# C v of a Nystrom attention in 64x32 tiles, each head by itself, in two parts a batch, under a newly planned order

## The chip, the cores and the metric

One core of a Trainium2 chip. The time is that of the core in device microseconds (us), from three runs, of which the median is given. One execution more was taken by the hardware profiler; its span runs from the first to the last instruction of the program. The engines are PE (TensorE, with PEld for its weight loads), DVE (VectorE), ACT (ScalarE), POOL (GpSimd) and SP (SyncE, which here only issues DMAs). Each takes its instructions in program order from a queue of its own.

## The reference

Batch 8, 8 heads, 576 positions of 64. Landmarks are means over 18 neighbouring positions, 32 per head. A = softmax(q k_lm'), B = softmax(q_lm k_lm'), C = softmax(q_lm k'), each over its last axis.

```python
Z = Bm.transpose(0, 1, 3, 2) / (norm1(Bm) * norminf(Bm) + 1e-06)   # over the last two axes
for _ in range(6):
    Z = 2 * Z - Z @ Bm @ Z
attn = A @ Z @ C @ v                       # 8 x 8 x 576 x 64
x = attn.transpose(0, 2, 1, 3).reshape(4608, 512)
out = ((x @ w1) * (x @ w2) @ w3) @ w_out   # 4608 x 512, float32
```

## The kernel before, in words

**Stages.** Heads are taken four at a time ("quads", two a batch, 16 in all). For a quad, POOL loads k and q as float16 (`lq`), DVE transposes them (`T`), the means go to `mk` and `lt` (PE for the first two quads, POOL for the rest: `ma`, `mb`). `S` is the product of q_lm and k with its softmax in `sm`, `sw`, `sb`, `se`; `ct` transposes its exponentials into `ecT`. `A` is the product of q and k_lm, with its softmax in `ar`, `am`, `as`, `ae`, `au`, `an`; `aT` is its transpose. Per group of one or two batches `N`, `x`, `Z` do the iteration of the reference.

**C v.** Per batch, `C` (`cv_mm`, L647) multiplies `ecT` by v (float32, loaded by SP as `lv` into `vb`). The 576 keys lie in two halves of 32 partitions a head and nine chunks; a product contracts 64 partitions. Two heads stand beside one another: the 64 columns of the weights are the 32 landmarks of two heads, and the streamed 128 columns are v of the same two heads. So of the 64x128 result only the two blocks of a head with itself are of use. Four such products, of two quads and two pairs, lie on the four 64x64 tiles of the array and in two PSUM banks. A tenth step multiplies the row sums of the exponentials by `unit64`, a scaled identity. `co` (`cv_out`, L665) divides by the sums and writes `cv` to SBUF. `W` (L755) multiplies `cv` by Z's block matrix; its view of `zb` takes the heads of each half in turn. `wp` and `wq` split W's result into two float16 parts and `U` multiplies it by w1 and w2, so that the two products with x become products `d` of aT with `u`.

**The dense part.** w3 and w_out are multiplied beforehand into `w34` (`mm`, 64 tasks of three products, after loads `w3n`, `wf` and splits `wh`, `wl`, `woh`, `wol`). `d` (16 matmul and weight-load instructions) gives both factors, `e` on ACT copies one, `f` on DVE multiplies. `g` (two halves of 8 instructions a tile of output) multiplies by w34, `h` on ACT copies, `st` on SP stores. `wu0` to `wu3` are six products each without use, at the start.

**The order.** The text `ORDER` (L39) names every task once, in the order in which its instructions are written to the engines' queues; behind a colon stand the buffers (PSUM banks, SBUF slots) that the task takes. It is the output of a planner that isn't in the file. What is left of it are the arguments of `add`: the planned occupation of the engine, the needs (`deps`), the buffers taken and given back (`acq`, `rel`), and `n`, the number of PE instructions. They don't change the program that is built from a given text, except through `acq`, which say which buffer a number belongs to.

A float32 product is two pairs of records in the trace (a weight load and a matmul each), a float16 product one pair.

## Time and profile before

| | |
|---|---|
| three runs | 277.85, 283.53, 285.95 us; median 283.53 |
| profiled execution | 276.25 us |
| its span | 274.5 us |
| PE busy | 93% of the span, 3948 matmul records |
| PE weight loads | 61% |
| DVE busy | 71% |
| ACT busy | 59% |
| POOL busy | 48% |
| C's products with v | 576 records, 272 ns each |

Busy shares are unions of the records of an engine. Matmuls are pipelined and lie over one another, so a record's length is longer than its share of the engine's time: what a stretch of PE's work takes is read from the start of its first record to the start of the next task's. "Issue" as the cause of an idle time means that nothing the profile shows was waited for. The granted TensorE clock was 0.995 over the span.

### The profile page before, as it was taken

The page shows a single profiled execution, that of the slowest core. Times are in us where ns is not written, and L with a number is a line of the kernel's source. Part 1 is how long each engine was busy: PE and PEld are TensorE (multiplying, and loading weights), DVE is VectorE, ACT ScalarE, POOL GpSimd, SP SyncE. Part 2 cuts the span into 40 slices and gives each one's busy share as a digit, 9 for nine tenths or more (in the row PEclk, how much of TensorE's full clock was granted, in tenths as well). Part 3 has the DMA queues.
Part 4 walks back from the last instruction along what each step waited for, and adds up shares of the span by engine and source line. Part 5 has one row for each costly group of instructions (what it writes and reads, how often), then busy time and mean ns, then how long its engine had stood idle before and what let it go on. Part 6 is the DMA issues. An engine that isn't in the chain of part 4 may idle for free.

```text
span 274.5 us, 9549 instructions
## 1 busy us (share of the span) xinstructions
PE 255.6 (93%) x3948; PEld 167.4 (61%) x3948; DVE 194.2 (71%) x470; ACT 161.3 (59%) x414; POOL 132.8 (48%) x147
## 2 busy tenths in 40 slices
PE   0958999999999899979999999999999999999993
PEld 0424444444658775568876647878866687557762
DVE  4489999999999999979999876757461255124330
ACT  0364563466477656969767799815129674485541
POOL 4006899999999889988979733000110000000000
PEclk9999999999999999999999999999999999999998
DMA  7997999999996964910476645254113210503636
GB/s 178 285 223 161 186 238 227 235 255 215 226 213 148 233 121 75 199 48 2 73 124 161 162 108 148 57 138 116 39 41 91 68 42 0 135 3 87 146 90 142
DMA packets 22668, 37.33 MB, mean 136 GB/s; under 512 B 3552, under 2 KB 7904, under 8 KB 22624
## 3 DMA queue, kind: packets, MB, share of 16 engines
q1 hardware_dynamic: 15920, 23.80, 35.2%
q0 software_dynamic: 5696, 11.54, 23.8%
q10 hardware_dynamic: 1008, 1.38, 1.7%
q8 instruction: 31, 0.51, 0.8%
q14 instruction: 13, 0.11, 0.1%
HBM read 38.80 MB, written 9.44 MB: 176 GB/s over the span
## 4 chain that ended last, share of the span: by engine, by line
PE 75%; DMA 16%; DVE 4%; issue 2%; ACT 1%; SPq 0%; DVEq 0%; ACTq 0%
PE bank L243 75%; DMA w3n<-in_moe_w_dram 13%; DMA u<-in_moe_w_out_dram 3%; DVE bank L325 1%; DVE tiny L498 1%; DVE w3t L340 1%; DVE ea L541 1%; DVE T L432 0%; ACT wo L314 0%; ACT lm L468 0%; DVE tiny L547 0%; DVE tiny L567 0%; ACT ec L517 0%; DVE T L474 0%; SPq L306 0%
## 5 line engine op out<-in xcount | busy, mean ns | idle before, releaser
L872 DVE TENSOR_TENSOR ab<-asb,bank 128x384 f16<-128x384 f16 x96 | 49.9, 544 | 38.8 <-ACT asb L866 38.3
L243 PE MATMUL bank<-aT,u 128*128 128x192 f16 x768 | 71.5, 246 | 0.0
L243 PE MATMUL bank<-w,ab 128*128 128x512 f16 (+1 forms) x296 | 69.9, 374 | 0.0
L243 PEld LDWEIGHTS <-u 128*128 128x128 f16 x768 | 63.6, 98 | 8.9 <-issue 1.3
L866 ACT CAST asb<-bank 128x384 f16<-128x384 f32 x96 | 44.1, 488 | 37.4 <-PE bank L243 29.4
L243 PE MATMUL bank<-wo,w3t 128*128 128x512 f16 x192 | 46.2, 379 | 3.7 <-ACT wo L314 2.3
L447 POOL TENSOR_TENSOR ls<-ls 128x128 f32<-128x128 f32 (+2 forms) x56 | 40.8, 729 | 4.0
L243 PEld LDWEIGHTS <-ab 128*128 128x128 f16 x296 | 27.6, 99 | 23.8 <-issue 0.7
L791 ACT CAST u<-bank 128x512 f16<-128x512 f32 x64 | 34.6, 615 | 5.7 <-PE bank L243 5.6
L581 POOL TENSOR_TENSOR ah<-ea,tiny 128x576 f16<-128x576 f32 x16 | 18.6, 1163 | 37.5 <-DVE aT L590 34.8
L440 POOL TENSOR_TENSOR ls<-nat 128x1152 f32<-128x1152 f16 x14 | 33.3, 2381 | 1.5 <-issue 1.0
L243 PEld LDWEIGHTS <-w3t 128*128 128x128 f16 x192 | 17.7, 99 | 23.8 <-issue 6.1
L886 ACT ACTIVATE osb<-bank 128x512 f32<-128x512 f32 x35 | 21.1, 607 | 16.9 <-PE bank L243 15.9
L553 POOL TENSOR_TENSOR ea<-ea,tiny 128x608 f32<-128x608 f32 x16 | 19.8, 1239 | 9.4 <-DVE tiny L547 4.8
L432 DVE STREAM_TRANSPOSE T<-nat 128x576 f32<-128x576 f32 x32 | 24.0, 751 | 0.1
L243 PE MATMUL bank<-T 32*32 32x288 f16 (+1 forms) x320 | 19.0, 291 | 0.7 <-DVE T L474 0.5
L517 ACT ACTIVATE ec<-bank,tiny 128x288 f32<-128x288 f32 x32 | 16.0, 504 | 5.2 <-DVE tiny L509 5.2
L243 PE MATMUL bank<-vb,ecT 64*64 64x128 f32 x576 | 18.3, 272 | 0.0
L243 PE MATMUL bank<-xz 32*32 32x64 f32 (+1 forms) x768 | 17.2, 214 | 1.1 <-issue 1.0
L243 PEld LDWEIGHTS bank<-vb,ecT 64*64 64x64 f32 x576 | 16.5, 133 | 1.9 <-ACT ec L517 0.9
L243 PEld LDWEIGHTS bank<-xz 32*32 32x32 f32 x768 | 12.9, 104 | 7.4 <-issue 4.2
L243 PE MATMUL bank<-w,wT 64*32 64x512 f16 x512 | 17.1, 379 | 0.0
(77 smaller groups left out, 296.0 us busy)
## 6 DMA issues: line engine op xcount, KB each, us to landing
vb<-in_v_dram SPq DMA_DIRECT2D x64, 144.0 KB, 3.9
out_dram<-osb SPq DMA_DIRECT2D x70, 128.0 KB, 2.4
nat<-in_k_dram POOLq DMA_DIRECT2D x16, 288.0 KB, 6.9
nat<-in_q_dram POOLq DMA_DIRECT2D x16, 288.0 KB, 7.5
w3n<-in_moe_w_dram SPq DMA_DIRECT2D x30, 128.0 KB, 8.0
w<-in_moe_w_dram POOLq DMA_DIRECT2D x4, 512.0 KB, 14.4
u<-in_moe_w_out_dram SPq DMA_DIRECT2D x4, 128.0 KB, 7.1
u<-in_moe_w_out_dram ACTq DMA_DIRECT2D x4, 128.0 KB, 7.2
```

What stands on the lines that cost most here:

```text
L243: nc.tensor.matmul(out_, lhsT, rhs, start=start, stop=stop, **({} if pos is None else {"tile_position": pos}))
L325: nc.vector.transpose(out=bank(at(f"w3f{j}{h}")).rearrange("p (e g i) -> p g e i", e=4, g=4), in_=w3n[at(f"w3n{j}")].rearrange("p g (e x) ...
L432: nc.vector.transpose(out=Ts[at(f"T{n}")][:, GRP * t:GRP * t + GRP] .rearrange("p r l e -> p (r l e)").bitcast(FP32), in_=nats[at(f"nat{n} ...
L440: nc.gpsimd.tensor_tensor(out=l, in0=nat[:, :, 0:9, :], in1=nat[:, :, 9:18, :], op=ALU.add)
L447: nc.gpsimd.tensor_tensor(out=l[:, :, x:x + m, :], in0=l[:, :, x:x + m, :], in1=l[:, :, y:y + m, :], op=ALU.add)
L517: nc.scalar.activation(out=ecs[at(f"ec{n}")][:, hp, :], in_=two(f"pS{n}")[hp][:, 0:288], func=AXF.Exp, scale=SCALE, bias=t[:, 2 + hp:3 + h ...
L553: nc.gpsimd.tensor_tensor(out=ea, in0=ea, in1=tinies[at(f"ta{n}")][:, 0:19].unsqueeze(2).to_broadcast([128, 19, M]), op=ALU.subtract)
L581: nc.gpsimd.tensor_tensor(out=ahs[at(f"ah{n}")].rearrange("p g m r -> p g r m"), in0=eas[at(f"ea{n}")][:, 0:GRP, :].rearrange("p (g r) m - ...
L791: nc.scalar.copy(out=uu[at(f"u{b}{qd}")][:, wi, 512 * half:512 * half + 512], in_=bank(at(f"pU{b}{wi}{half}{qd}")))
L866: nc.scalar.copy(out=asb[at(f"as{b}{j}{ch}")], in_=d1_ps(b, j, ch)[0])
L872: nc.vector.tensor_mul(abts[at(f"ab{i // 2}")][:, 2 * j:2 * j + 2, CH * (i % 2):CH * (i % 2) + CH], asb[at(f"as{b}{j}{ch}")], d1_ps(b, j, ...
L886: nc.scalar.activation(out=osb[at(f"os{i}")], in_=bank(at(f"pE{i}")), func=AXF.Copy, scale=2.0 ** -12)
```

## The change

C is computed head by head: weights of 32 columns, 64 streamed columns of v, eight products a step on the eight 64x32 tiles. The useless blocks fall away, the number of products doubles. The ten steps are written as two tasks, `Cba` (steps 0 to 4) and `Cb` (5 to 9), which the order may set apart; both use the same two banks. `cv` and `unit64` have half the width, `co` multiplies 64 columns instead of 128, and `W` is two products of 128 streamed columns instead of four of 64, without the reordering view. `ORDER` is a new text from beginning to end: 1336 words instead of 1328, with other places for the loads, the warm-up products and nearly all other tasks, and other buffers. Some of the planner's figures changed too (occupations of `wu`, `C`, `co`; DMA times of `lq` and `lw`).

```diff
-    cvs = slots(fixed, 2, [128, 2, 2, D], FP32, "cv")
+    cvs = slots(fixed, 2, [128, 2, D], FP32, "cv")
-    unit64 = fixed.tile([128, 64], FP32, name="unit64")
+    unit64 = fixed.tile([128, 32], FP32, name="unit64")
...
-    def cv_mm(b):
+    def cv_mm(b, c0, c1):
         def fn():
             ps = two(f"pC{b}")
-            for c in range(NC9 + 1):
+            for c in range(c0, c1):
                 for qd in range(2):
                     n = 2 * b + qd
                     for h2 in range(2):
-                        r, o = slice(64 * (h2 ^ qd), 64 * (h2 ^ qd) + 64), 64 * h2
-                        if c < NC9:
-                            mm(ps[qd][o:o + 64, 0:128],
-                               ecTs[at(f"ecT{n}")][r, c, :, :].rearrange("p a m -> p (a m)"),
-                               vbs[at(f"vb{n}")][r, :, c, :],
-                               start=(c == 0), stop=(c == NC9 - 1), pos=(r.start, o))
-                        else:
-                            mm(ps[qd][o:o + 64, 128:130], unit64[r, :], tinies[at(f"mx{n}")][r, 4:6],
-                               pos=(r.start, o))
+                        r = slice(64 * (h2 ^ qd), 64 * (h2 ^ qd) + 64)
+                        for a in range(2):
+                            o = 64 * h2 + 32 * a
+                            if c < NC9:
+                                mm(ps[qd][o:o + 32, 0:D], ecTs[at(f"ecT{n}")][r, c, a, :], vbs[at(f"vb{n}")][r, a, c, :],
+                                   start=(c == 0), stop=(c == NC9 - 1), pos=(r.start, o))
+                            else:
+                                mm(ps[qd][o:o + 32, D:D + 1], unit64[r, :], tinies[at(f"mx{n}")][r, 4 + a:5 + a],
+                                   pos=(r.start, o))
...
-                rc = tinies[at(f"tc{b}")][:, 2 * qd:2 * qd + 2]
-                nc.vector.reciprocal(out=rc, in_=ps[:, 128:130])
-                nc.vector.tensor_tensor(out=cvs[at(f"cv{b}")][:, qd],
-                                        in0=ps[:, 0:128].rearrange("p (a d) -> p a d", a=2),
-                                        in1=rc.unsqueeze(2).to_broadcast([128, 2, D]), op=ALU.mult)
+                nc.vector.reciprocal(out=t[:, qd:qd + 1], in_=ps[:, D:D + 1])
+                nc.vector.tensor_tensor(out=cvs[at(f"cv{b}")][:, qd], in0=ps[:, 0:D],
+                                        in1=t[:, qd:qd + 1].to_broadcast([128, D]), op=ALU.mult)
...
-            for x in range(2):
-                for s in range(2):
-                    zb = zbs[at(f"zb{i}")][:, 2 * b - 2 * GROUPS[i][0] + s, :, :]
-                    mm(ps[64 * s:64 * s + 64, 0:128].rearrange("p (e a m) -> p a e m", e=2, a=2)[:, x], cvs[at(f"cv{b}")][:, s, x, :],
-                       zb.rearrange("p (e a) m -> p a e m", a=2)[:, x], pos=(0, 64 * s))
+            for s in range(2):
+                mm(ps[64 * s:64 * s + 64, 0:128], cvs[at(f"cv{b}")][:, s, :],
+                   zbs[at(f"zb{i}")][:, 2 * b - 2 * GROUPS[i][0] + s, :, :].rearrange("p h m -> p (h m)"), pos=(0, 64 * s))
...
-        add(f"C{b}", "PE", 2.2, cv_mm(b), deps=[f"ct{n0}", f"ct{n1}", f"lv{n0}", f"lv{n1}", "cc"],
-            acq=both(f"pC{b}", 1),
+        add(f"C{b}a", "PE", 0.89, cv_mm(b, 0, 5), deps=cvd, acq=both(f"pC{b}", 1),
             rel=[f"ecT{n0}", f"ecT{n1}", f"vb{n0}", f"vb{n1}", f"mx{n0}", f"mx{n1}"],
-            at=(p, 2.0), mode="64x64", kind="C", n=160)
+            at=(p, 2.0), mode="64x32", kind="C", n=160)
+        add(f"C{b}", "PE", 0.89, cv_mm(b, 5, 10), deps=[f"C{b}a"],
+            rel=[f"ecT{n0}", f"ecT{n1}", f"vb{n0}", f"vb{n1}", f"mx{n0}", f"mx{n1}"],
+            at=(p, 2.1), mode="64x32", kind="C", n=160)
```

The new order around C1, C2 and C3 (excerpts; the words of PE's tasks begin with mm, C, A, S, d, x, sw, N, Z, W, U, g):

```
C1a:2.4 wo7 ae6 T81 A7:1.3 se61 f010 lq100:2 d011:6.0 ar7:1 mb8
d021:5.7 e011:2 ct5:1 x1_0:1 e021:0 au6 C1 f021 S7:3.6 lv6.0:2 f011 d020:5.7
...
d012:0.1 lv6 am7:1 an6:1 C2a:2.4
...
d002:0.5 T90:1 ma9:0 ae7 C2 sb7 f020 e002:2 au7 se70:1 lv8.0:0 d031:7.0
...
Z1:6 sb9 C3a:7.5 zo1:1 se81 ma11:0 f022 ae9 W2:6 ct8:1 W1:0 se90:1 g30:4 au9
```

The start of the new order (the warm-ups are wu0 to wu3):

```
tr00:0.0 wf3s zz wh00 tr01:1 wu0:2 wf2a T00:0 wh01 w3n1.0:1 woh0 gw0 w3n1.1 mp0:3 T01
woh1 wl01 wf3a.0 wu1:4 wol0 mk0:0 w3n1.2 wol1 wf3a lt0 wl00 T10:1 woh3 gw1 w3n1 A0:5.6 woh2 S0:7.2 wol3 wu3:1
ar0:0 w3n2.0:2 sm0:0 mm00:3 am0:1 mp1:0 woh5 w3n2.1 T11 as0 woh4 mm01 wol5 w3n2.2 mk1:1 sw0 wol4 gw2 wu2:4 gw3
```

## The prediction

> **What bounds the kernel now.** I read the page first, then the chain that ended last, then PE's waits.

> ```profile
> span 274.5 us, 9549 instructions
> PE 255.6 (93%) x3948; PEld 167.4 (61%) x3948; DVE 194.2 (71%) x470; ACT 161.3 (59%) x414; POOL 132.8 (48%) x147
> q8 instruction: 31, 0.51, 0.8%
> ```

> The columns of the chain are start, length and what held it.

> ```profile
> 61.78 28.72 PE bank L243 x561
> 90.50 0.86 issue
> 91.37 6.31 PE bank L243 x128
> 97.67 0.16 issue
> 97.84 19.31 PE bank L243 x370
> 117.15 1.41 issue
> 118.56 151.13 PE bank L243 x2367
> ```

> From 61.78 us to PE's last product the chain is PE alone, but for two holes named "issue". So PE's own work and PE's holes set the time. DVE is nearly as full until 160 us, as the stretches show (after the time: PE, PEld, DVE, ACT, POOL busy, granted clock, DMA share, GB/s):

> ```profile
> 28.00:60.00 32.00, 31.93 (x289) 14.69 (x287) 30.78 (x69) 16.37 (x46) 30.18 (x35) 1.00 1.10 230
> 60.00:118.00 58.00, 55.91 (x1107) 36.40 (x1106) 55.56 (x139) 39.42 (x115) 54.81 (x56) 1.00 0.86 180
> 118.00:160.00 42.00, 41.45 (x794) 30.91 (x794) 38.68 (x92) 32.01 (x92) 33.62 (x35) 1.00 0.44 98
> 160.00:275.00 115.00, 109.67 (x1660) 77.45 (x1658) 50.35 (x122) 63.50 (x141) 5.87 (x5) 0.99 0.34 83
> ```

> **What the holes are.** Queue 8 brought 31 packets of instructions; PE's 3948 matmul and 3948 weight-load records make 7896, or 255 a packet. The two holes end at 91.37 and 118.56:

> ```profile
> 91.36:118.50 27.14, 25.61 (x509) 17.18 (x509) 25.72 (x59) 18.82 (x54) 25.11 (x26) 1.00 0.73 151
> ```

> Between them PE ran 509 + 509 records, and with the few semaphore instructions that is four times 256. So PE runs through blocks of 256 instructions, and a hole is a block that had not come when the one before was used up. Counting from these two points, every block boundary of the trace can be placed. Four blocks of about 256 records:

> ```profile
> 82.18:85.58 3.40, 3.40 (x136) 3.40 (x131) 3.26 (x11) 3.38 (x10) 3.32 (x5) 1.00 0.43 94
> 85.58:91.36 5.78, 4.92 (x139) 3.66 (x131) 5.17 (x17) 3.15 (x9) 5.46 (x7) 1.00 1.00 215
> 112.45:118.55 6.10, 4.70 (x144) 2.99 (x129) 5.93 (x15) 4.87 (x12) 5.87 (x6) 1.00 0.81 186
> 195.76:198.80 3.04, 3.04 (x143) 2.93 (x133) 1.24 (x4) 0.00 (x0) 1.16 (x1) 1.00 0.02 5
> ```

> The second and third end with the hole, so there a fetch took 5.78 and 6.10 us from the entry into a block to the next one's use, with the DMA engines 81% to full. The first passed without a hole in 3.40 us, the fourth, with idle DMA engines, in 3.04. In the third the packet began only after 116 us, behind data:

> ```profile
> q1 hardware_dynamic: 119, 0.21, 61.6%
> q0 software_dynamic: 28, 0.03, 19.1%
> q8 instruction: 1, 0.02, 5.6%
> ```

> (This is the stretch from 116 to 117 us; from 112.4 to 116 the same view has no queue 8.) My measure is thus: a block that PE uses up faster than **L** costs the difference. L is at least 3.4 and at most 6.1 us while inputs stream in (to about 118 us); I take the middle, 4.8. Later I take 3.0, from the block at 195.76.

> **C itself.** A C before, and what follows it:

> ```profile
> 112.97 2.20 PE L243 MATMUL bank<-vb,ecT 64*64 64x128 f32 x72
> 114.99 0.24 PE L243 MATMUL bank<-tiny,unit 64*64 64x2 f32 x8
> 115.16 0.63 PE L243 MATMUL bank<-w,wT 64*32 64x512 f16 x16
> ```

> From 112.97 to 115.16: 2.19 us for 80 records, 8 times 17.5 us. After, a batch has 160 records: ten steps (nine chunks of keys and the unit step) of eight products of one head each, where there were four of a pair of heads, and still two records a product. A record streams 64 columns instead of 128, and eight tiles of the array work side by side instead of four, so streaming falls to about half or less and the price of starting a record decides. Rows of small records:

> ```profile
> 95.02 0.49 PEld L243 LDWEIGHTS bank<-xz 32*32 32x32 f32 x32 [0.16 <-DVE ab L872]
> 107.19 0.14 PEld L243 LDWEIGHTS <-wT 64*32 64x32 f16 x16 [0.24 <-issue]
> L243 PE MATMUL bank<-minus2I,xz x32: 191/191/191, 103.3 to 103.9; 32*32 32x32 f32 x32
> ```

> x starts 32 records in 0.49 us (15.3 ns each, with four tiles in use, so streaming is in it), U's loads 16 in 0.14 (8.8), and Z, whose 32 records of this row alternate with 32 more, 64 in 0.6 (9.4). I take 11 ns, near Z, the nearest in type: 160 x 11 = 1.76 us a batch, 0.88 a half. Saved: 8 x (2.19 - 1.76) = **3.4 us**; with 8.8 ns it is 6.3, with 15.3 a loss of 2.1. [...]

> W's product loses half its 8 records, 4 x 9.4 ns x 8 = 0.3 us; I count **0.2**. On DVE the multiply of co halves its width:

> ```profile
> L670 DVE TENSOR_TENSOR cv<-bank,tiny 128x128 f32<-128x128 f32 x16 | 4.7, 292 | 0.6
> L706 DVE TENSOR_TENSOR xz<-bank,tiny 128x64 f32<-128x64 f32 x2 | 0.4, 224 | 0.1
> ```

> 16 x 68 ns is 1.1 us of DVE, behind PE's work: nothing. The smaller cv and unit tiles cost nothing. Bank pairs are held over both halves, longer than before; all eight banks are rotated by the written order, and I take no wait from it, at most one of 1 us.

> **More fetches, shorter blocks.** PE gets 8 x 80 more records and loses 8 x 4: 4556, with loads 9112, so 36 packets instead of 31. A C is 320 instructions, more than a block, so each of the eight has a boundary in it or at its end. I laid the new order's PE words out at 256 instructions a block, with spacings from the trace; for d (8 + 8 instructions) and g (4 + 4) from

> ```profile
> 240.13 1.03 PE L243 MATMUL bank<-w,ab 128*128 128x512 f16 x4
> 241.00 0.82 PE L243 MATMUL bank<-aT,u 128*128 128x192 f16 x8
> 241.66 1.03 PE L243 MATMUL bank<-w,ab 128*128 128x512 f16 x4
> ```

> 0.87 for g, 0.66 for d; x of two batches 0.5, Z 0.6 as above. The short blocks come out so: C0's second half with three and a half products of the weights, 3.9 us; most of C1 with A7, two d and an x, 3.2; the rest of C1, S7, two d, half of C2a, 2.8; the rest of C2 with one d, 2.3; Z1 and C3a, 1.6; C3 with two g and two U, 4.3; C5 with W4 and W3, 2.1; C7 alone with the end of C7a, 1.5. C4's is 4.1, C6's over 4. With L 4.8 up to C3 and 3.0 after: 0.9 + 1.6 + 2.0 + 2.5 + 3.2 + 0.5 and 0.9 + 1.5 = 13.1 us. Before paid, on the same account (the weight loads in order of time, and PE's waits in total):

> ```profile
> 91.37 0.16 PEld L243 LDWEIGHTS bank<-xz 32*32 32x32 f32 x8 [1.02 <-issue]
> 118.56 0.10 PEld L243 LDWEIGHTS bank<-bm,ones 32*32 32x32 f32 x2 [1.68 <-issue]
> PE bank L243 <- issue: 2.4, 3, 1.4
> ```

> PE's three waits are 2.4 us; the two holes seen from the loads 2.7, which I take. Net **+10.4**. With L of 3.4 and 3.0 the sum is 6.2, net +3.5; with 6.1 and 3.4 about 22, net +19. The boundaries can lie some tens of instructions off, since semaphore instructions are spread evenly in my count; that moves single blocks by a few tenths of a us.

> **Start and end.** PE before 31 us (excerpt):

> ```profile
> 14.78 0.38 PE L243 MATMUL bank<-wo,w3t 128*128 128x512 f16 x1 [1.32 <-ACT wo L314]
> ...
> 17.68 0.38 PE L243 MATMUL bank<-wo,w3t 128*128 128x512 f16 x1 [0.94 <-ACT wo L314]
> ...
> 28.82 0.52 PE L243 MATMUL bank<-T 32*32 32x288 f16 x16
> 29.27 1.47 PE L243 MATMUL bank<-aT 128*128 128x512 f16 x6
> ```

> The last row is a warm-up without use, 1.3 us of a stretch where PE is otherwise full. In the new order all four warm-ups stand ahead of the third product, where PE waits on ACT and DVE anyway. S1 comes earlier as well, but DVE then has sm0, am0 and T11 ahead of its weight halves. I take the 1.3 us as gained and nothing else: **-1.3**, between -2.2 and +1.5. The loads of q, k and w12 change places in POOL's queue by one or two words; cb moves ahead of two loads, which delays those by its 0.3 us, while DVE has T0 to do. At the end the last store is a whole tile (0.6 us on ACT instead of 0.38, two issues after it instead of two or three): nothing, within 0.7.

> **The sum.** -3.4 - 0.2 + 10.4 - 1.3 = +5.5 us against the profiled execution's 276.25, so 281.8, 2.0% more: slower, on the edge of what can be told. That execution is the fastest of four (276.25, 277.85, 283.53, 285.95, mean 280.9; median of the three 283.53). I add to the mean: **286.4**.

> **The rivals.**
> *Longest fetches.* If every fetch while inputs stream takes the 6.1 us of the block at 112.45, and 3.4 later, net fetch is +19: +14, slower by 5%. It decides from L of about 5. For it: two of the blocks that could tell showed 5.8 and 6.1. Against it: 82.18 passed in 3.40.
> *Fetches hidden.* With L of 3.4 and 3.0 the sum is -1.4; if the packets come in time everywhere and the old holes go too, -3.4 - 0.2 - 1.3 - 2.7 = -7.6, faster. It decides where L stays under the 1.5 to 2.8 us of the shortest blocks, or where the written order has PE waiting there anyway. [...]
> *DVE holds the stage to 160 us.* At 55.56 of 58 us it may set the pace there, so that PE's holes and C's gain before it both count for nothing. Left are three C (-1.3), the late fetches (+2.4) and the start: about 0.
> *Starting a record costs x's 15.3 ns.* Then C loses 2.1 instead of gaining 3.4: +11.0 at most, slower, since longer halves also shorten the fetch holes. [...]

> **How the numbers follow.** A measurement of this kernel can tell about 2%, 5.6 us, from no change. Forecast 0.38 (from +1 to +10: 0.19 within 2%, 0.19 slower); longest fetches 0.22, slower; hidden 0.22 (0.14 faster, 0.08 within); DVE 0.11, within; price of starting 0.07, slower. Together faster 0.14, same 0.38, slower 0.48. The range runs from 276.5 (hidden fetches, part) to 296 (longest fetches, and the scatter of the four times); the forecast's own is 282 to 291.

> **What would show it.** Queue 8 with about 36 packets; PE's "issue" waits of 8 us or more in all, the longest around C1, C2, C3 and C7; C's 80 records of a half within 0.9 us where no hole falls in; the third product later, but no warm-up after 25 us. I am wrong if "issue" stays at 2 to 4 us, if a half takes over 1.1 us without a hole, or if PE's longest waits become those on DVE.

## The result, and the profile after

The changed kernel takes 287.49 us (median of four runs, 285.92 to 293.46), the kernel before 280.69 beside it (four runs, 277.06 to 285.95). The ratio is **1.0319** with a 95% interval of 1.0249 to 1.0389: slower. The forecast was 286.4 us, 2.0% more. The profiled execution took 285.92 us, 9.7 more than that of before. The ratio compares the undisturbed executions alone, so it isn't the quotient of the two medians; the 293.46 us, for one, ran at a granted clock of 0.968 and is left out.

The page of the changed kernel, parts 1, 2 and 3 (in part 2 each digit is a fortieth of the span):

```profile
span 284.0 us, 10784 instructions
PE 255.2 (90%) x4556; PEld 164.2 (58%) x4556; DVE 193.9 (68%) x470; ACT 161.6 (57%) x414; POOL 132.9 (47%) x147
PE   0887999988999499899999989999979999999992
PEclk9999999997999979999999999999999999999997
q8 instruction: 35, 0.57, 0.9%
```

PE's busy time is the old one within half a us; the span is 9.5 us longer. So PE's work did not grow, its holes did. Four more packets of instructions were brought, 35 instead of 31. Twice the granted clock falls to 0.50 while PE works, for 3.41 us each, in slices 10 and 15 (the 7 at the end lies behind PE's last product; before had an 8 there).

The chain that ended last (start, length, holder), in excerpts:

```profile
64.48 0.49 issue
64.97 13.56 PE bank L244 x110
...
98.64 1.27 issue
99.92 16.91 PE bank L244 x333
116.83 0.80 issue
...
127.61 0.73 issue
...
163.07 1.33 issue
164.41 42.58 PE bank L244 x896
206.98 1.55 issue
208.53 45.95 PE bank L244 x574
254.51 24.22 PE bank L244 x191
```

Before 128 us the chain now also runs through DVE; whether DVE or something else held PE there, the chain alone can't tell. The pieces named "issue" stand each ahead of a restart of PE. The weight loads in order of time show them whole (start, length, instructions; in brackets the idle time before):

```profile
64.98 0.19 PEld L244 LDWEIGHTS bank<-zb,cv 128*64 128x64 f32 x3 [2.35 <-issue]
93.44 0.48 PEld L244 LDWEIGHTS bank<-vb,ecT 64*32 64x32 f32 x38 [0.53 <-issue]
99.91 1.09 PEld L244 LDWEIGHTS <-u 128*128 128x128 f16 x8 [4.03 <-issue]
117.63 0.41 PEld L244 LDWEIGHTS bank<-zb,cv 128*64 128x64 f32 x6 [0.93 <-issue]
128.34 0.13 PEld L244 LDWEIGHTS <-T 32*32 32x32 f16 x12 [0.92 <-issue]
164.41 0.12 PEld L244 LDWEIGHTS <-T 32*32 32x32 f16 x11 [1.54 <-issue]
208.53 0.13 PEld L244 LDWEIGHTS <-wT 64*32 64x32 f16 x11 [1.85 <-issue]
```

Seven holes, 12.15 us, where the kernel before had two with 2.70. They lie behind C0 (in W0), in C2's first half, behind C2, behind C3's first half, in the product S11, behind C5 and behind C7. In the trace, counted by their starts, each comes 193 or 194 records of PE past a multiple of 256 (weight loads, products and the semaphore instructions between them), as both holes of before did. So do, from C0 on, all holes of 0.9 us or more of the runs below, in every one.

A trap in the reading: in PE's list of waits, the hole at 64.97 is put down to another engine.

```profile
PE bank L244 <- issue: 8.7, 6, 3.9
PE bank L244 <- DVE w3t L339: 2.4, 1, 2.4
```

The work that starts at 64.97 is W0 (operands `zb,cv`), which does not use w3t; what it needs was ready, by the chain, at 61.8 us (`61.46 0.33 DVE zb L745`), and its first weight load had run at 62.49. The 2.4 us belong to the fetch. A wait's name tells what ended last among the things that the profile takes for a cause, and a fetch is not among them.

C itself is as small as hoped. C1's halves (start, length, instructions):

```profile
86.20 1.04 PE L244 MATMUL bank<-vb,ecT 64*32 64x64 f32 x80
87.17 0.72 PE L244 MATMUL bank<-T 128*128 128x320 f16 x4
...
89.72 0.80 PE L244 MATMUL bank<-vb,ecT 64*32 64x64 f32 x60
...
90.61 0.45 PE L244 MATMUL bank<-T 32*32 32x288 f16 x16
```

0.97 and 0.89 us from start to next start, 1.86 a batch against 2.19.

### The profile page after: what moved, and what is told of

Same layout as the page of the kernel before. It is cut to its first block, busy times and chain, and to the rows that moved or that the text cites. A ratio compares the mean times of both kernels' runs of the same rounds, so it can differ in the third digit from the quotient of the medians.

```text
span 284.0 us, 10784 instructions
## 1 busy us (share of the span) xinstructions
PE 255.2 (90%) x4556; PEld 164.2 (58%) x4556; DVE 193.9 (68%) x470; ACT 161.6 (57%) x414; POOL 132.9 (47%) x147
## 4 chain that ended last, share of the span: by engine, by line
PE 67%; DMA 17%; DVE 9%; issue 4%; SPq 1%; ACT 0%; ACTq 0%; DVEq 0%
PE bank L244 67%; DMA w3n<-in_moe_w_dram 11%; DMA ab<-in_moe_w_out_dram 2%; DMA vb<-in_v_dram 2%; DMA u<-in_moe_w_out_dram 2%; DVE tiny L546 1%; DVE tiny L497 1%; DVE bank L324 1%; DVE ea L540 1%; DVE tiny L566 1%; DVE T L431 1%; DVE ab L871 1%; DVE w3t L339 1%; DVE cv L669 1%; SPq L305 1%
## 5 line engine op out<-in xcount | busy, mean ns | idle before, releaser
L871 DVE TENSOR_TENSOR ab<-asb,bank 128x384 f16<-128x384 f16 x96 | 49.3, 544 | 45.1 <-ACT asb L865 40.3
L244 PEld LDWEIGHTS <-u 128*128 128x128 f16 x768 | 64.6, 99 | 12.1 <-issue 6.4
L244 PE MATMUL bank<-w,ab 128*128 128x512 f16 (+1 forms) x296 | 68.7, 374 | 0.0
L244 PE MATMUL bank<-wo,w3t 128*128 128x512 f16 x192 | 47.4, 387 | 2.8 <-DVE wo L318 2.8
L244 PE MATMUL bank<-T 32*32 32x288 f16 (+1 forms) x320 | 19.7, 293 | 3.9 <-issue 2.1
L244 PE MATMUL bank<-w,wT 64*32 64x512 f16 x512 | 18.1, 379 | 1.6 <-issue 1.5
L331 ACT ACTIVATE w3t<-bank 128x512 f16<-128x512 f32 x16 | 9.4, 593 | 12.6 <-DVE bank L324 10.1
L244 PEld LDWEIGHTS <-T 32*32 32x32 f16 (+1 forms) x320 | 8.7, 91 | 13.3 <-issue 7.1
```

Source lines behind the costliest of these rows:

```text
L244: nc.tensor.matmul(out_, lhsT, rhs, start=start, stop=stop, **({} if pos is None else {"tile_position": pos}))
L331: nc.scalar.activation(out=w3t[at(f"w3t{j}")][:, 0, 4 * h:4 * h + 4].rearrange("p e g i -> p (e g i)"), in_=bank(at(f"w3f{j}{h}")), func=A ...
L871: nc.vector.tensor_mul(abts[at(f"ab{i // 2}")][:, 2 * j:2 * j + 2, CH * (i % 2):CH * (i % 2) + CH], asb[at(f"as{b}{j}{ch}")], d1_ps(b, j, ...
```

## Experiments

Three theories stood against one another. **Fetch:** PE uses up blocks of 256 instructions faster than they come, so what counts is where the boundaries fall in the program. **Order:** the new order has waits or banks of its own that cost the time. **DVE:** DVE sets the pace to 160 us and hides PE's holes.

**The order of before with the new form.** Each word `Cb` was replaced by `Cba Cb`.

```diff
-lq81 ae4 zo0:0 lv3.2 ma6:0 lt5 mm67 wh70 tr71:2 bo3 A5:4.1 sb4 wl70 wh71 lv3 se40:1 au4 C0:0.7 mb6 ar5:1 T61
+sw4 mm66 lq81 ae4 zo0:0 lv3.2 ma6:0 lt5 mm67 wh70 tr71:2 bo3 A5:4.1 sb4 wl70 wh71 lv3 se40:1 au4 C0a:0.7 C0 mb6 ar5:1
```

> The order of before, word for word, with each word C replaced by the two halves next to each other, in the form of the change (64x32 tiles, one head a product). Theory (PE waits for blocks of instructions): counted on the order of before, a block that holds both halves is used up in 1.5 us, and with fetches of 5.2 us while inputs stream and 3.3 later the holes add up to some 18 to 26 us, where the kernel before has 2.7. With 3.4 to 3.6 saved in C that is 292 to 300 us by the profile's 276. Rival (the new order is at fault, by waits on other engines or by its banks, and the form is not): 272 to 274 us, faster than before.

Measured 304.74 us (before 278.66), ratio 1.1005 (1.0907 to 1.1102). PE's waits and the granted clock:

```profile
PE bank L239 <- issue: 21.2, 9, 4.0
PEclk9968999999796699967999999998999799999999
```

Nine holes behind or in the C's, 22.6 us in the loads' rows, within the 18 to 26 counted beforehand from the order's text alone. The clock falls behind several of them (its mean is 0.937), a cost that the count did not have; the time is past the range. So the form isn't rescued by the old order; it is far worse in it, since both halves stand side by side there.

**The new order with the form of before.**

```diff
...
-                            if c < NC9:
-                                mm(ps[qd][o:o + 32, 0:D], ecTs[at(f"ecT{n}")][r, c, a, :], vbs[at(f"vb{n}")][r, a, c, :],
-                                   start=(c == 0), stop=(c == NC9 - 1), pos=(r.start, o))
...
+                        if c < NC9:
+                            mm(ps[qd][o:o + 64, 0:128],
+                               ecTs[at(f"ecT{n}")][r, c, :, :].rearrange("p a m -> p (a m)"),
+                               vbs[at(f"vb{n}")][r, :, c, :],
+                               start=(c == 0), stop=(c == NC9 - 1), pos=(r.start, o))
...
```

> The changed kernel's order, with C, co and W in the form of before (64x64 tiles, a pair of heads a product), C still in two parts (steps 0 to 4 and 5 to 9). PE has 3948 matmul records again. Theory: the holes fall from 13 us to about 1 to 3, the two stretches of half clock behind the longest holes (3.4 us each, so 1.7 lost in each) go, C takes 3.5 more: 274 to 278 us, the level of before or a little under it. Rival (order at fault): 284 us or more, as the changed kernel, plus up to 3.

Measured 277.45 us, ratio 1.0006 (0.9968 to 1.0045). The first rows of PE's waits:

```profile
PE bank L244 <- DVE aT L262: 6.6, 1, 6.6
PE bank L244 <- DVE wo L320: 3.1, 2, 1.8
PE bank L244 <- DMA nat<-in_q_dram: 1.6, 1, 1.6
```

No row of "issue" is left, and no hole at a boundary. The order theory falls as the cause of the 3%: this order is as fast as the old one. It isn't faster either, though it lacks the old one's 2.7 us of holes, so its other waits cost about as much more. Some 2 us of them lie at the start: C0's first product starts at 60.18 us, in the changed kernel at 58.15. The rest was not followed up.

**Only the boundaries moved.** The warm-ups stream the same columns in more products, so that everything behind them lies 192 or 48 PE instructions later. The diff is that of 192; for 48 there are 12 products of 256 columns.

```diff
-        for _ in range(WARM):
-            mm(bank(at(f"pwu{x}")), aTs[0][:, 0:128], aTs[0][:, 0:512])
+        for _ in range(30):
+            mm(bank(at(f"pwu{x}"))[:, 0:104], aTs[0][:, 0:128], aTs[0][:, 0:104])
```

> The changed kernel with each of the four warm-ups written as 30 products of 104 columns instead of 6 of 512: the same streamed columns, 192 PE instructions more, all before the first use of the weights' products. Nothing else changes, but every boundary of a block of 256 lies 192 instructions earlier in the program. Theory: holes by my count 9 us instead of 15 (measured 13), so 4 to 6 us less, and one stretch of half clock less: 278 to 282 us. Rival (holes come from the work at their place, not from the place of the boundary): 285 to 287 us and holes at C2, C3, C7 as before the shift.

Measured 279.17 us, ratio 1.0059 (1.0004 to 1.0114). The weight loads' holes that are left:

```profile
93.25 0.15 PEld L244 LDWEIGHTS bank<-vb,ecT 64*32 64x32 f32 x6 [0.53 <-issue]
99.72 0.26 PEld L244 LDWEIGHTS bank<-xz 32*32 32x32 f32 x16 [2.23 <-issue]
133.81 0.24 PEld L244 LDWEIGHTS <-T 128*128 128x128 f16 x3 [1.95 <-issue]
```

4.7 us instead of 12.15, and none behind C0, C3, C5 or C7. One stretch of half clock is left, of two.

> The same with 12 products of 256 columns a warm-up: 48 PE instructions more, boundaries 48 earlier. Theory: holes by my count 22 us instead of 15, so 5 to 7 us more: 291 to 295 us. Rival: 285 to 287 us.

Measured 295.63 us, ratio 1.0642 (1.0533 to 1.0751), with 14.5 us of "issue" waits on PE and a mean granted clock of 0.969. Two kernels with the same work in the same order, 144 instructions of warm-up apart, differ by 16 us, and by more than the change itself. The rewritten warm-ups are not the reason, for C0 starts at 60.30 us with the shift by 192 and at 60.01 with that by 48. That settles the fetch theory.

It also bears against DVE as the pace-maker, though not wholly. From C0 to C4 (whose first products start at 145.53 and 151.93 us) the shift by 48 loses 6.7 us on that by 192. On PE alone it would be 7.9: its holes there are 4.7 us longer, and PE works 10.0 us at half clock instead of 3.4. In the same way that by 192 gains 3.7 of 5.7 us on the changed kernel (58.15 to 147.03). So most of such a cost comes through, and a sixth to over a third is taken up by other waits. Behind C4, 7.2 of 7.5 us come through.

**A mixture.** Batches 0 to 3 in the old form, 4 to 7 in the new, with the warm-ups of the shift by 48.

```diff
+PAIRED = (0, 1, 2, 3)
...
-        add(f"C{b}a", "PE", 0.89, cv_mm(b, 0, 5), deps=cvd, acq=both(f"pC{b}", 1),
+        add(f"C{b}a", "PE", 0.89, (cv_mm if b in PAIRED else cv_mm_one)(b, 0, 5), deps=cvd, acq=both(f"pC{b}", 1),
...
```

> The new order with the form of before (pairs of heads, 64x64) in batches 0 to 3, whose halves lie in the stretch where inputs stream in, and the form of the change in batches 4 to 7; warm-ups as 12 products of 256 columns, so that boundaries lie 48 instructions earlier, where my count has the smallest sum of holes, 1.1 us (3.1 without the shift). Theory: no hole over 1 us, four C at 0.45 us less than in the run with the old form throughout: 274.5 to 276.5 us, about 1% under the kernel before. Rival (the new form costs more than its holes, or switching between forms costs PE): 277.5 us or more.

Measured 274.65 us (before 277.75), ratio 0.9888 (0.9857 to 0.9919): a gain of 1.1%, small but clear of its interval, within the range expected. One "issue" wait of 0.4 us is left on PE.

**Why a fetch is long.** At C7 the DMA engines move nothing but the instructions. Stretch of the changed kernel from the entry into the block to the restart, and the only queue at work in it (in the second row the stretch ahead of the hole behind C3's first half, where queue 8 is alone too):

```profile
205.41:208.53 3.12, 1.57 (x146) 1.27 (x133) 0.84 (x2) 0.40 (x2) 0.00 (x0) 1.00 0.02 5
114.79:117.63 2.84, 2.04 (x147) 1.77 (x138) 2.15 (x5) 2.03 (x7) 2.23 (x1) 1.00 0.02 6
```

```profile
q8 instruction: 1, 0.02, 2.1%
```

So a fetch without company took 2.8 and 3.1 us. At C0 it was 6.4 us, with the engines full:

```profile
58.58:64.98 6.40, 3.99 (x145) 2.43 (x139) 6.30 (x16) 3.10 (x9) 6.11 (x10) 1.00 1.10 236
```

Three runs took data away.

> The changed kernel with a ninth of v loaded: each of the 64 loads brings the first of nine chunks (16 KB instead of 144), the rest of v's buffers is cleared once by GpSimd early, where it waits for a weight load. The products with v are all issued; their result is not the reference's. PE's stream of instructions is the same, word for word. Theory (a fetch takes 5 to 6 us because its packet waits behind data): with 8 MB less of 37 the engines are freer from 60 to 130 us, the holes at C0, C2, C3 and C4 shrink; by a fetch of 3.3 us everywhere the sum is 6 us instead of 13, so 276 to 281 us with less half clock. Rival (the length of a fetch doesn't depend on the data loaded): the same holes within 1 us, 284 us or more.

```diff
+    def clear_v():
+        for x in vbs:
+            nc.gpsimd.memset(x.rearrange("p a c d -> p (a c d)"), 0.0)
...
-            nc.sync.dma_start(out=vbs[at(f"vb{n}")][p0:p0 + 32].rearrange("p a c d -> p a (c d)"),
-                              in_=src[s ^ qd, t])
+            nc.sync.dma_start(out=vbs[at(f"vb{n}")][p0:p0 + 32][:, :, 0, :], in_=src[s ^ qd, t][:, :, 0:D])
```

Measured 287.99 us, ratio 1.0372 (1.0321 to 1.0422): no gain. C2's hole fell from 4.03 to 2.11, but C0's grew from 2.35 to 2.90 and the late ones to 1.99 and 2.15. The run also has a fault of its own, below: PE's first product starts 4.8 us later, and C0 2.2. So it was repeated without the clearing, for quads 4 to 15 only:

```diff
-            nc.sync.dma_start(out=vbs[at(f"vb{n}")][p0:p0 + 32].rearrange("p a c d -> p a (c d)"),
-                              in_=src[s ^ qd, t])
+            nk = NC9 if n < 4 else 1
+            nc.sync.dma_start(out=vbs[at(f"vb{n}")][p0:p0 + 32][:, :, 0:nk, :].rearrange("p a c d -> p a (c d)"),
+                              in_=src[s ^ qd, t][:, :, 0:nk * D])
```

> The changed kernel with a ninth of v loaded from the fifth quad on, in place of the run with cleared buffers, whose start was late by 2 us of its own (a DVE cast took 5.1 us beside GpSimd's clearing). The result is not the reference's; PE's stream is the same. Theory (queue 0 is what a packet waits behind, v on queue 1 adds little): the hole at C0 stays at 2 us or more, C2's loses 1 to 2 us, sum 10 to 12 us: 282 to 285 us. Rival (any data in the same amount count alike): as the run with small k and q loads, 275 to 280 us.

Measured 286.84 us, ratio 1.0399 (1.0323 to 1.0476). C2's hole is 1.83 instead of 4.03, C0's is 2.46, the late ones are 2.29 and 2.19:

```profile
66.35 0.19 PEld L244 LDWEIGHTS bank<-zb,cv 128*64 128x64 f32 x3 [2.46 <-issue]
99.95 1.27 PEld L244 LDWEIGHTS <-u 128*128 128x128 f16 x16 [1.83 <-issue]
163.02 0.13 PEld L244 LDWEIGHTS <-T 32*32 32x32 f16 x11 [2.29 <-issue]
```

The holes are 11.2 us in all, within the expected 10 to 12, and yet the time is just above the range. The starts of the same products tell why. C0 starts 1.2 us later than in the changed kernel (59.34), C4 1.9 us earlier (145.18), so the gain at C2 is there. Then C5's hole, 2.29 instead of 1.54, is followed by half clock (0.50 from 163.10 to 166.51 us), which the changed kernel's was not, and C7's is 0.34 longer; that takes the gain back.

```diff
+            nr = GRP if n < 4 else 2
...
-                out=nats[at(f"nat{n}")][:, t, :, :],
-                in_=(k, q)[t][b, 4 * qd:4 * qd + 4].rearrange("h (l r) d -> (h l) r d", r=GRP))
+                out=nats[at(f"nat{n}")][:, t, 0:nr, :],
+                in_=(k, q)[t][b, 4 * qd:4 * qd + 4].rearrange("h (l r) d -> (h l) r d", r=GRP)[:, 0:nr])
```

> The changed kernel with a ninth of k and q loaded from the fifth quad on (2 of 18 rows of each landmark's positions; the rest of a buffer keeps what an earlier quad brought, so the result is not the reference's). PE's stream is the same. These loads run on queue 0, which GpSimd issues and which converts to 16 bits. In the changed kernel the instruction packet came 3.6 to 4.4 us after the entry into the block where queue 0 moved 65 to 143 GB/s, and 0.2 to 1.6 us after it where only other queues or none were at work. Theory (the packet waits behind queue 0): from 60 to 130 us packets start within 2 us, fetches take 3 to 4 us, the hole at C0 (2.5 us) goes, that at C2 (4.1) falls to 1 to 2, the sum to 6 to 8 us with at most one stretch of half clock: 275 to 280 us. Rival (data don't matter): holes within 1 us of the changed kernel's, 284 us or more.

Measured 282.87 us (before 276.80), ratio 1.0205 (1.0128 to 1.0283), between theory and rival. Three of its holes:

```profile
63.78 0.19 PEld L244 LDWEIGHTS bank<-zb,cv 128*64 128x64 f32 x3 [0.57 <-issue]
95.43 2.02 PEld L244 LDWEIGHTS <-u 128*128 128x128 f16 x16 [2.38 <-issue]
203.49 0.13 PEld L244 LDWEIGHTS <-wT 64*32 64x32 f16 x11 [1.85 <-issue]
```

C0's hole falls from 2.35 to 0.57, C2's from 4.03 to 2.38, S11's is gone; the late ones stay to the hundredth. The holes are 7.7 us in all instead of 12.15. So data in flight do lengthen a fetch, in the changed kernel from 2.8 and 3.1 us up to 6.4 at C0, and with few k and q loads over a third of the holes' length is gone. What is left behind C3's first half and at C7 stands on idle DMA engines. Whether queue 0 counts more than queue 1 stays open: each of the three runs shortened C2's hole by some 2 us, while C0's became shorter with k and q alone, on whose queue the loads of w1 and w2 ran as well.

## The prediction, step by step

*PE's own work and its holes set the time:* right in the main; PE is busy for 255.2 us after 255.6, and the time went up and down with the holes and the half clock behind them. But before C4 a sixth to over a third of such a cost is taken up by other waits, as the shifts show.

*Holes are blocks of 256 instructions that come late:* right; all seven lie 193 or 194 records past a multiple of 256, and the shifts show it.

*Their sum, 13.1 us:* 12.15 in the loads' rows. The sum fits better than its parts. By place, expected and measured: C0 0.9 and 2.35, C1 1.6 and 0, from C1 to C2 2.0 and 0.53, C2 2.5 and 4.03, C3 3.2 and 0.93, behind it 0.5 and 0.92, C5 0.9 and 1.54, C7 1.5 and 1.85. So that the sum is right is in part luck. The 4.8 us taken for every fetch while inputs stream stood for fetches of 2.8 to 6.5, and C3's, the 2.8, fell in a pause of the loads. The late 3.0 was right to 0.1 at C7, but at C5 3.8 passed from the entry to the restart. One reading behind these figures does not hold: a block that passes in 3.40 us without a hole shows that its fetch took no longer than that; it gives no least length.

*C at 11 ns a record, 3.4 us saved:* 1.86 us a batch instead of 1.76, so 8 x 0.33 = 2.6 us by C1. The step is right and its size over a quarter too large. The mixture gains 1.1% with half of it. *W, 0.2:* W0 takes 0.38 us with four records (64.97 to 65.35), as it did with eight before (77.46 to 77.84); nothing came of it.

*The start, 1.3 us won:* right in this profile. Products of the weights that PE had started by 32.49 us, before and after:

```profile
0.00:32.49 32.49, 9.14 (x35) 1.00 0.94 206
```

```profile
0.00:32.49 32.49, 10.33 (x42) 1.00 1.03 226
```

Seven more, 1.5 us of work, with all warm-ups done in both. It isn't steady: in the profiles of the old form in the new order, of the two shifts and of the mixture they are 36 or 37.

*The end, nothing within 0.7:* from PE's last product (chain, 254.51 + 24.22) to the end 5.3 us, before 4.8.

*What the sum lacked:* it came to +5.5 for a measured +9.7 of the profiled executions. The half clock behind the two longest holes is the term that has no place in it:

```profile
65.71:69.12 3.41, 3.41 (x12) 1.45 (x10) 3.31 (x9) 1.66 (x5) 3.31 (x4) 0.50 1.14 248
99.90:103.25 3.35, 3.33 (x43) 2.92 (x47) 0.48 (x2) 1.18 (x3) 2.65 (x5) 0.50 1.09 237
```

In each PE did about half of what it does otherwise: from their start to the next start, 16 products with x took 2.67 us at 99.92, and 1.34 at 133.85. By an estimate from that and the granted 0.50, 1.7 us were lost in each, 3.4 in both. With it and the terms as measured (12.15 - 2.70 for the holes, -2.6, -1.5, +0.5 at the end) the sum is +9.3; the 0.4 left is not assigned. Since the shifts show that before C4 not all of a hole's cost comes through, so close a fit is in part luck too. And that the forecast of 286.4 us lies so near the measured 287.49 has a second reason: the 5.5 us were added to 280.9, the mean of four times of before of which two were over 283. The change itself came out 9.7 in the profiles, not 5.5.

*The rivals:* longest fetches came at C0 and C2, 6.4 and 6.5 us (58.58 to 64.98, 93.44 to 99.91), and nearly at S11, 5.9; in C2's first half and behind C3's it was only 3.5 and 2.8, so +14 did not come. Hidden fetches: 12 us of holes contradict them; only the run with the old form in this order has none. DVE as the pace-maker to 160 us is contradicted by the shifts, except for the part named above. The price of starting was no cause: a half took 0.89 us.

## What to carry to other kernels

On an engine that is always busy, count its instructions as well as its time: here the fetches that left a hole took from 2.8 us, with the DMA engines otherwise idle, to 6.5 while inputs streamed in, and a stretch of 256 PE instructions that was done sooner than its fetch cost the difference. A form with smaller products that halves the streaming can lose for that alone; use it where long products stand around it and DMA engines are idle (the mixture, with the new form in batches 4 to 7 alone, gained 1.1%), and move the boundaries by a few dummy instructions before an order is judged, since 144 of them were worth 16 us here. A fetch theory can be tested on a trace alone: count PE's records up to each hole and see whether they agree modulo 256.

## What had not been expected of the hardware

In these runs a hole could cost more than its length. In the changed kernel those of 2.35 and 4.03 us were followed by 3.41 us of half granted clock, those of 1.54 and 1.85 were not; in the second run with small loads of v one of 2.29 was followed, one of 2.19 was not. Nor does its length decide: with the order of before a hole of 1.78 us was followed (140.62), in the first run with small loads of v one of 2.90 was not (67.27).

```profile
62.30:65.71 3.41, 1.00 (x8) 1.00 1.10 241
205.66:209.07 3.41, 1.86 (x139) 1.00 0.02 5
```

```profile
62.09:65.50 3.41, 2.56 (x19) 1.00 0.97 181
65.50:68.91 3.41, 1.95 (x13) 1.00 0.98 141
68.91:72.32 3.41, 3.41 (x18) 1.00 1.10 203
```

So in these traces a hole cost another 1.7 us, by the estimate above, when it left PE without a product for 1.78 us or more of one such piece, and with 1.61 to 1.70 in three cases of seven.

A DVE copy took 5.13 us where the same instruction takes 0.23, while GpSimd cleared four buffers beside it. First the run with cleared buffers, DVE and POOL, then DVE of the changed kernel:

```profile
2.93 5.13 DVE L275 CAST ident<-ident 128x128 f16<-128x128 f32 x1 [1.93 <-POOL ident L253]
3.89 4.08 POOL L270 MEMSET vb<- 128x1152 f32 x4
```

```profile
2.92 0.23 DVE L274 CAST ident<-ident 128x128 f16<-128x128 f32 x1 [1.92 <-POOL ident L258]
```

It ended 0.1 us after the last of the clearings. So in this run clearing on GpSimd went with a DVE copy that ended 4.9 us later, and with a later start of the kernel. By these rows the copy starts before the clearings, but spans on POOL are rough; how the two met is not shown.
